# A new order, new engine places and new buffer slots for a two-layer attention and MLP kernel on one core

## The chip, the core and the metric

The kernel runs on one core of a Trainium2 chip. A core has five engines with queues of their own: TensorE (PE in the profile; PEld is its weight load), VectorE (DVE), ScalarE (ACT), GpSimd (POOL) and SyncE (SP, which here issues transfers). Each engine works through its own instructions in program order and waits on semaphores for the others. The metric is the device time of one execution in microseconds (us); a smaller number is better.

## The reference

The input x (2048 tokens, 512 wide, bfloat16) passes twice through an attention layer A and a gated MLP layer B with the same weights:

```
def A(x):                                  # 32 heads of 16
    q, k, v = heads(layernorm(x) @ wqkv)
    pq, pk = q @ w_phi, k @ w_phi          # per head, 16 x 16
    phi_q = concat(softmax(pq), softmax(-pq));  phi_k = concat(softmax(pk), softmax(-pk))
    kv, z = phi_k^T @ v, sum(phi_k)        # over all tokens
    return (phi_q @ kv / (phi_q @ z + 1e-6)) @ wo
def B(x):
    gate, up = layernorm(x) @ W_gate, layernorm(x) @ W_up     # 512 -> 1376
    return (relu(gate) * up) @ W_down
x = x + A(x);  x = x + B(x);  x = x + A(x);  x = x + B(x)
```

Since kv and z are sums over all tokens, no query of a layer can be finished before the keys of all 16 tiles of that layer are.

## The kernel before

The tokens are 16 tiles of 128. x stays in on-chip memory (X0 to X3, four tiles each) through both layers. The work on a tile in layer A is: statistics (L508, L509), the inverse deviation on ACT (L516, L518), the normalised tile (L532 on DVE or L530 on POOL), a transpose (by a DMA at L493, in pairs of tiles, or for a few tiles by PE at L498 with a copy at L451 on ACT or L452 on DVE), then keys (K, L600) and values (V, L605). Before the first keys the kernel folds w_phi into the key and query weights (L471 and L479 on PE; the folded block matrix Wblk comes from L427). The keys are exponentiated on ACT (`ek`, L572), summed on DVE (L610), inverted through a logarithm and an exponential on ACT (L619, L622), scaled on DVE or POOL (L559), and multiplied with the values (L633) into one sum for all tiles; L645 and L650 make the matrix R of it on DVE.

A query goes the same way: Q (L660), exponentials (L572), a sum on DVE (L665), its inverse on ACT (L670, L672), a ratio on DVE (L676), a scaling on DVE or POOL (L681), and a DMA transpose into a buffer `fq` (L685). PE then multiplies it with R (L696, called `erq` below, "the read of a query"); the denominator is inverted (L705 on DVE, or L703 and L707 on ACT), the result divided (`o`, L710 on DVE), transposed by DMA in pairs of tiles (`oT`, L493; L498 by PE for the first tiles) and projected with wo (L719); L723 adds it to x.

Layer B takes blocks of 1, 1, 2, 4, 4, 2, 2 tiles in the first layer and 1, 1, 2, 4, 4, 2, 1, 1 in the second. A block is centred (L739), transposed (`xnTB`, L493), and multiplied with gate and up weights (L796; L772 does the last 96 columns for both, whose product `hr` is transposed by a DMA at L823 into the buffer `hT`). ACT takes the relu (L800); the product with up is made on DVE straight from PSUM (L813) or, after a copy of up by ACT (L815), from on-chip memory (L804). The sum of squares is taken on ACT (L745) or on DVE (L747). L836 multiplies with W_down, L843 adds to x, and in the second layer L909 stores the tile.

All of this is recorded first as 1882 operations. Three tables, found beforehand by a search and written into the file, then decide how they run:

- `ORDER` is the order in which the recorded operations are emitted; each engine's own program is that order cut down to its operations.
- `PLACE` has one digit for each operation that two engines can do, and says whether it goes to the other one (POOL or DVE for L427, L530/L532, L559 and L681; ACT or DVE for copies out of PSUM, the product of gate and up, the sum of squares and the denominators; the SP or ACT queue for a few loads).
- `SLOTS` says which buffer of its pool each operation takes: six PSUM banks `b`, seven `fq`, three `xn`, two `o`, three `oT`, and so on. A later user of a slot waits for the former one's last reader.

All transposes, nearly all loads and all stores are issued from SP, in one queue: an issue that waits for its input holds up every one behind it.

Of the kernel before, what the change touches and what calls it, by code (L numbers as in the profile page):

```python
# [145 lines left out]
class K:  # L146
# [9 lines left out]
    "1100101010111011000101001001110000010000110100110101011100110100011100000001000001110111001100010011"  # L156
    "1011110010100110100110101100110010000011011000100110000101000000000000000010011101011011010000001111"
    "0110100011101101110101110000000000111100101110110100110101000000011111100110000101111000110000101110"
    "0000100111111000101101011000101101111011000011010111100"
)  # L160
SLOTS = (
    "0001451253130010000013433322441511022214304534304520050102235401411130832125312102411256331270021370"
    "4314410132122a2009024c310d231b142h251i001a160j315f152c0209233g122e344k001d36000505011414020002510110"
    "2031000011100000200102101214001021540100022005020051044205021251402023121002134234005118130100014100"
    "2202135243040120423155003011400413211322102300425203200113411011250122634200130057121522132001013152"
    "0101100530350341111442332040341322131322140103k3135j4101150021153235201052103215i3413442210011100400"
    "020112511430024103022325032b063h232a104i354j212c0219345b232c364e203h220a335f0419364g112d150115040202"
    "1200101212020000200110211000001242011020510000120100015021011410003214302515421031152025013100015005"
    "2133051131225042310241140520100300510201110131221041032244530110101030112103012251121021125251220055"
    "30120011510440022320332204103111211515311001500000542450235"  # L170
# [784 lines left out]
```

## Time and profile before

| what | value |
|---|---|
| median of 3 runs | 371.1 us (370.42 to 371.11) |
| the profiled execution | 371.12 us, of which the span of the instructions is 369.1 us |
| PE busy | 362.4 us, 98% of the span |
| DVE busy | 260.5 us, 71% |
| ACT busy | 197.3 us, 53% |
| POOL busy | 70.0 us, 19% |
| granted TensorE clock | 0.999 of full speed, mean |
| moved by DMA | 31.73 MB, of it 0.36 MB and 0.11 MB on the two queues that the page calls instruction |

A profile row names a line of the kernel, an engine, an operation, and what it writes and reads (out<-in, buffer numbers left out). A row of the timeline begins with the start of the first instruction and the time it covers, both in us; the bracket at its end gives the idle time of the engine before it and what ended it. "SPq" is an issue on SP's queue, its second number the time that the issue took. Times of PE overlap: a matmul of 512 columns lasts 379 ns from start to modelled end, while the next one begins 216 ns after it.

### The profile page before, as it was taken

The numbers are of one execution on the slowest core, as the hardware profiler recorded it, in microseconds if no ns is written. First come the engines' busy times: TensorE is split into PE (matmuls) and PEld (weight loads), VectorE is DVE, ScalarE is ACT, GpSimd is POOL, SyncE is SP. The second block draws the span as 40 slices with busy tenths as digits, with TensorE's granted clock in tenths as the row PEclk, the third lists the DMA queues.
The fourth block names the chain that finished last, engine by engine and source line by source line (L and its number), as shares of the span: only waits on it lengthen the run. The fifth ranks groups of instructions, "written<-read, shape, count | busy, mean of one in ns | idle before, by whom it ended". The sixth has DMA issues, their size and how long they took to land.

```text
span 369.1 us, 7462 instructions
## 1 busy us (share of the span) xinstructions
PE 362.4 (98%) x2845; PEld 217.2 (59%) x2845; DVE 260.5 (71%) x598; ACT 197.3 (53%) x562; POOL 70.0 (19%) x99
## 2 busy tenths in 40 slices
PE   8989999999999999999999999999999999999996
PEld 5545567776455544456767455777744444466684
DVE  6989999999667457657959878898845823432343
ACT  5989998645256531655555477854422431323231
POOL 4688930320200000003002671040010000000000
PEclk9999999999999999999999999999999999999999
DMA  7998486556544400221012611156861110202013
GB/s 221 252 191 204 180 133 126 106 114 142 115 89 73 95 1 2 44 66 28 2 36 59 143 30 30 29 117 133 138 118 30 43 28 2 57 16 65 16 46 119
DMA packets 93923, 31.73 MB, mean 86 GB/s; under 512 B 85344, under 2 KB 92864, under 8 KB 93888
## 3 DMA queue, kind: packets, MB, share of 16 engines
q1 hardware_dynamic: 93888, 31.26, 38.6%
q8 instruction: 22, 0.36, 0.4%
q14 instruction: 13, 0.11, 0.1%
HBM read 8.44 MB, written 2.10 MB: 29 GB/s over the span
## 4 chain that ended last, share of the span: by engine, by line
PE 84%; DMA 7%; DVE 4%; SPq 2%; ACT 1%; issue 1%
PE b L796 34%; PE b L836 18%; PE b L719 7%; PE b L605 6%; PE b L600 6%; PE b L660 6%; PE b L772 2%; DMA fq<-ek 2%; PE q L633 2%; DMA oT<-o 2%; PE q L696 2%; DMA xnTA<-xn 1%; DVE sq L665 1%; DMA X<-in_A_x_dram 1%; PE b L498 1%; DVE X L723 1%
## 5 line engine op out<-in xcount | busy, mean ns | idle before, releaser
L796 PE MATMUL b<-xnTB,wgu 128*128 128x128 bf16 (+2 forms) x1200 | 153.4, 279 | 0.0
L796 PEld LDWEIGHTS <-wgu 128*128 128x128 bf16 x1200 | 97.4, 98 | 46.1 <-issue 0.2
L800 ACT ACTIVATE gu<-b 128x512 bf16<-128x512 f32 (+1 forms) x83 | 47.5, 581 | 105.9 <-PE b L796 104.6
L836 PE MATMUL b<-wd,hT 128*128 128x512 bf16 (+3 forms) x363 | 85.2, 373 | 0.1
L572 ACT ACTIVATE ek<-b 128x480 bf16<-128x480 f32 x128 | 68.9, 580 | 12.8 <-PE b L600 6.7
L813 DVE TENSOR_TENSOR hT<-gu,b 128x512 bf16<-128x512 bf16 (+1 forms) x49 | 32.8, 671 | 38.2 <-PE b L796 19.0
L836 PEld LDWEIGHTS <-hT 128*128 128x128 bf16 (+1 forms) x363 | 34.6, 98 | 35.5 <-DMA hT<-hr 0.6
L681 POOL TENSOR_TENSOR ek<-ek 128x480 bf16<-128x480 bf16 x19 | 18.6, 990 | 158.2 <-DVE ek L676 82.5
L559 POOL TENSOR_TENSOR ek<-ek 128x480 bf16<-128x480 bf16 x39 | 38.7, 1016 | 34.2 <-ACT ek L622 33.6
L665 DVE TENSOR_REDUCE sq<-ek 128x64 f32<-128x960 bf16 x32 | 36.3, 1143 | 1.0 <-ACT ek L572 1.0
L610 DVE TENSOR_REDUCE sk<-ek 128x64 f32<-128x960 bf16 x32 | 36.0, 1142 | 1.0 <-ACT ek L572 0.7
L843 DVE SCALAR_TENSOR_TENSOR X<-b,rsB,X 128x512 bf16<-128x512 f32 (+2 forms) x33 | 24.1, 730 | 12.3 <-PE b L836 12.2
L723 DVE SCALAR_TENSOR_TENSOR X<-b,X 128x512 bf16<-128x512 f32 x32 | 21.7, 684 | 15.1 <-PE b L719 15.0
L719 PE MATMUL b<-wo,oT 128*128 128x512 bf16 x128 | 31.9, 379 | 0.5 <-DMA oT<-o 0.4
L605 PE MATMUL b<-wv,xnTA 128*128 128x512 bf16 x128 | 31.5, 379 | 0.0
L600 PE MATMUL b<-Wk,xnTA 128*128 128x480 bf16 x124 | 28.9, 366 | 1.7 <-DMA xnTA<-xn 1.7
L660 PE MATMUL b<-Wq,xnTA 128*128 128x480 bf16 x128 | 30.0, 366 | 0.0
L710 DVE TENSOR_TENSOR o<-q,rd 128x512 bf16<-128x512 f32 x32 | 22.0, 688 | 5.3 <-ACT rd L707 4.8
L508 DVE BATCH_NORM_STATS2 bstA<-X 128x6 f32<-128x512 bf16 x32 | 21.3, 682 | 2.0 <-DMA X<-in_A_x_dram 1.8
L815 ACT CAST gu<-b 128x512 bf16<-128x512 f32 (+1 forms) x34 | 18.8, 560 | 6.2 <-PE b L796 6.0
L804 DVE TENSOR_TENSOR hT<-gu 128x512 bf16<-128x512 bf16 (+1 forms) x34 | 13.6, 402 | 11.2 <-ACT gu L815 10.9
L600 PEld LDWEIGHTS <-xnTA 128*128 128x128 bf16 x124 | 11.7, 98 | 13.9 <-DMA xnTA<-xn 1.8
(81 smaller groups left out, 333.5 us busy)
## 6 DMA issues: line engine op xcount, KB each, us to landing
out_dram<-X SPq DMA_DIRECT2D x15, 128.0 KB, 1.8
X<-in_A_x_dram SPq DMA_DIRECT2D x6, 256.0 KB, 5.0
wgu<-in_B_W_gate_dram SPq DMA_DIRECT2D x4, 344.0 KB, 4.5
wgu<-in_B_W_up_dram SPq DMA_DIRECT2D x4, 344.0 KB, 5.8
wd<-in_B_W_down_dram SPq DMA_DIRECT2D x5, 256.0 KB, 3.6
hT<-in_A_wqkv_dram SPq DMA_DIRECT2D x4, 256.0 KB, 4.0
X<-in_A_x_dram SPq DMA_DIRECT2D x4, 128.0 KB, 3.0
wv<-in_A_wqkv_dram SPq DMA_DIRECT2D x2, 256.0 KB, 4.4
```

What stands on the lines that cost most here:

```text
L559: e.tensor_tensor(out=v[:, :, 0:DF, :], in0=v[:, :, 0:DF, :], in1=spread(ek, v, n), op=Alu.mult)
L572: nc.scalar.activation(out=pairs(ek, s)[:, :, 0:DF, :], in_=ps.t[:, 0:FW].rearrange("p (b f h) -> p b f h", h=2, f=DF), func=AF.Exp, scale ...
L600: k = op("PE", mm(4, FW), due, lambda: [nc.tensor.matmul(kp.t[:, 0:FW], lhsT=xnTA[c][:, i, b, :], rhs=Wk2[:, b, :], start=(b == 0), stop=( ...
L605: v = op("PE", mm(4, 512), due_v, lambda: [nc.tensor.matmul(vp.t[:], lhsT=xnTA[c][:, i, b, :], rhs=wv[:, b, :], start=(b == 0), stop=(b == ...
L610: a = op("DVE", SUM16, due, lambda: nc.vector.tensor_reduce(out=sk.t[:, row, :].rearrange("p (b h) -> p b h", h=2), in_=summed(pairs(ek)), ...
L660: q = op("PE", mm(4, FW), due, lambda: [nc.tensor.matmul(qp.t[:, 0:FW], lhsT=xnTA[c][:, i, b, :], rhs=Wq2[:, b, :], start=(b == 0), stop=( ...
L665: a = op("DVE", SUM16, due, lambda: nc.vector.tensor_reduce(out=sq.t[:].rearrange("p (b h) -> p b h", h=2), in_=summed(pairs(ek)), axis=AX ...
L719: a = op("PE", mm(4, 512), due + 3, lambda j=j, yp=yp: [nc.tensor.matmul(yp.t[:], lhsT=oT.t[:, j, b, :], rhs=wo[:, b, :], start=(b == 0), ...
L796: nc.tensor.matmul(ps.t[:, q * W:(q + 1) * W].rearrange("p (i t) -> p i t", t=P), lhsT=wgu[:, s, b, g * P:(g + 1) * P], rhs=xT.t[:, 0:n, b ...
L800: nc.scalar.activation(out=gu.t[:, 0, 0:cols], in_=gp.t[:, 0:cols], func=AF.Relu)
L813: nc.vector.tensor_tensor(out=h.t[:, f0 * W:f0 * W + cols], in0=gu.t[:, 0, 0:cols], in1=up.t[:, 0:cols], op=Alu.mult)
L836: nc.tensor.matmul(yp.t[:, 0:c1 - c0], lhsT=h.t[:m, f * W + i * P:f * W + (i + 1) * P], rhs=wd[:m, f, c0:c1], start=(f == 0), stop=(f == N ...
```

## The change

The three tables are replaced. No operation is added or removed, and no other line differs: the 2845 matmuls are the same ones, and so are the widths and the blocks. The first rows of each table:

```diff
 PLACE = (
-    "1100101010111011000101001001110000010000110100110101011100110100011100000001000001110111001100010011"
+    "1110001010101011000100001101110100010000110100000001011000010110001111001001000001011100001100001100"
...
 SLOTS = (
-    "0001451253130010000013433322441511022214304534304520050102235401411130832125312102411256331270021370"
+    "0001451040132010500014430222331211020213005544034243050301110131332321832325222114330207421163021150"
...
 ORDER = (
-    2, 16, 9, 29, 3, 21, 25, 0, 8, 4, 102, 1, 10, 103, 17, 19, 22, 104, 7, 105, 46, 30, 106, 32, 5, 31, 47, 6, 84, 48,
+    3, 16, 9, 29, 2, 0, 17, 19, 25, 8, 4, 1, 10, 102, 6, 103, 30, 46, 7, 104, 32, 105, 106, 31, 5, 47, 84, 48, 14, 49,
```

What `PLACE` moves, counted over the operations: 6 of 64 key scalings (L559) and 6 of 32 query scalings (L681) go from POOL to DVE; the block matrix Wblk (L427) goes from POOL to DVE; one normalised tile from POOL (L530) to DVE (L532); three sums of squares from ACT (L745) to DVE (L747); three products of gate and up from DVE alone (L813) to ACT and DVE (L815, L804); one more denominator goes to ACT; one weight load goes from the SP queue to the ACT queue. PE's program has as many instructions as before.

Three places show how the order differs. The first is the queue of SP at the start, from the last early load to the transpose of the second pair of tiles (`xn2` into `xnTA3`); `hT0` holds the query weights there, `hT1` their transpose. Before:

```order
L353 DMA wd_71<-in_B_W_down_dram 96x512
L493 DMA_TRANSPOSE xnTA1_80<-xn0_109 128x8x128
L869 DMA hT0_163<-in_A_wqkv_dram 128x2x512
L465 DMA_TRANSPOSE hT1_164<-hT0_163 128x8x128
L353 DMA wo_66<-in_A_wo_dram 128x512
L353 DMA X2_63<-in_A_x_dram 128x2x512
L493 DMA_TRANSPOSE xnTA3_82<-xn2_111 128x8x128
```

and now:

```order
L353 DMA wo_66<-in_A_wo_dram 128x512
L493 DMA_TRANSPOSE xnTA1_80<-xn0_109 128x8x128
L353 DMA X3_64<-in_A_x_dram 128x2x512
L869 DMA hT0_163<-in_A_wqkv_dram 128x2x512
L465 DMA_TRANSPOSE hT1_164<-hT0_163 128x8x128
L493 DMA_TRANSPOSE xnTA3_82<-xn2_111 128x8x128
```

Between the two transposes of x there are now three other issues and not four; the load of `wo` stands ahead of both.

The second place is on DVE, where the eighth `o` of the first layer is made; the seventh projection of PE waits for it. Before:

```order
L710 TENSOR_TENSOR o0_156<-q0_102,rd0_153 128x512
L843 SCALAR_TENSOR_TENSOR X0_61<-b1_104,rsB0_96,X0_61 128x512
L804 TENSOR_TENSOR hT1_164<-gu2_167 128x512
L676 SCALAR_TENSOR_TENSOR ek19_131<-sq3_145 128x16x2
L681 TENSOR_TENSOR ek19_131<-ek19_131 128x16x30
L676 SCALAR_TENSOR_TENSOR ek9_121<-sq2_144 128x16x2
L754 SCALAR_TENSOR_TENSOR sqB0_95<-ssq_84,lnB0_97 128x1
L676 SCALAR_TENSOR_TENSOR ek20_132<-sq0_142 128x16x2
L705 RECIPROCAL rd1_154<-q0_102 128x32
L781 TENSOR_TENSOR hr0_170<-gr1_169,b2_105 128x96
L710 TENSOR_TENSOR o0_156<-q0_102,rd1_154 128x512
```

and now:

```order
L710 TENSOR_TENSOR o0_156<-q0_102,rd0_153 128x512
L804 TENSOR_TENSOR hT0_163<-gu2_167 128x512
L532 TENSOR_SCALAR xn0_109<-X0_61,mvA1_92,rsA1_93 128x512
L751 TENSOR_TENSOR lnB0_97<-rowsum_83 128x2
L723 SCALAR_TENSOR_TENSOR X1_62,rowsum_83<-b2_105,X1_62 128x512
L747 SCALAR_TENSOR_TENSOR wasteD_86,ssq_84<-X0_61 128x512
L723 SCALAR_TENSOR_TENSOR X1_62,rowsum_83<-b5_108,X1_62 128x512
L754 SCALAR_TENSOR_TENSOR sqB0_95<-ssq_84,lnB0_97 128x2
L804 TENSOR_TENSOR hT0_163<-gu0_165 128x512
L705 RECIPROCAL rd1_154<-q0_102 128x32
L710 TENSOR_TENSOR o0_156<-q0_102,rd1_154 128x512
```

Between the seventh and the eighth `o` there are now two additions to x (L723), a sum of squares (L747) and a normalised tile of the next layer (L532), each 512 wide.

The third place is the queue of SP in the attention of the second layer, up to the transpose of the query of tile 11. That query goes into `fq3` before and into `fq5` now. Before:

```order
L493 DMA_TRANSPOSE oT2_160<-o0_156 128x8x128
L493 DMA_TRANSPOSE xnTB0_161<-xn1_110 128x8x128
L685 DMA_TRANSPOSE fq4_150<-ek15_127 128x8x128
L493 DMA_TRANSPOSE oT0_158<-o1_157 128x4x128
L493 DMA_TRANSPOSE xnTB0_161<-xn2_111 128x8x128
L493 DMA_TRANSPOSE oT1_159<-o0_156 128x4x128
L685 DMA_TRANSPOSE fq3_149<-ek10_122 128x8x128
```

and now:

```order
L685 DMA_TRANSPOSE fq3_149<-ek12_124 128x8x128
L685 DMA_TRANSPOSE fq6_152<-ek14_126 128x8x128
L685 DMA_TRANSPOSE fq5_151<-ek16_128 128x8x128
L493 DMA_TRANSPOSE oT0_158<-o0_156 128x8x128
L685 DMA_TRANSPOSE fq2_148<-ek11_123 128x8x128
L493 DMA_TRANSPOSE oT2_160<-o1_157 128x4x128
L493 DMA_TRANSPOSE xnTB0_161<-xn0_109 128x8x128
```

The transpose of that query stood behind three transposes of `o` and two of `xn` and was the last of the seven; it now stands ahead of both transposes of `o` and of the transpose of `xn` in the piece shown.

More of the change, by code (lines that the diff above doesn't have):

```diff
@@ L155 @@
 PLACE = (
-    "1100101010111011000101001001110000010000110100110101011100110100011100000001000001110111001100010011"
-    "1011110010100110100110101100110010000011011000100110000101000000000000000010011101011011010000001111"
-    "0110100011101101110101110000000000111100101110110100110101000000011111100110000101111000110000101110"
-    "0000100111111000101101011000101101111011000011010111100"
+    "1110001010101011000100001101110100010000110100000001011000010110001111001001000001011100001100001100"
@@ L160 @@
+    "1111010101001111110000100000110110011010010101100000100011000100100000011100111100010000100010111110"
+    "1110001011110100001010100000110011100100101001111100101100010101011011111000110100110110100111000100"
+    "0010000100011010011111011001000111111100101110100100001"
 )
 SLOTS = (
-    "0001451253130010000013433322441511022214304534304520050102235401411130832125312102411256331270021370"
-    "4314410132122a2009024c310d231b142h251i001a160j315f152c0209233g122e344k001d36000505011414020002510110"
@@ L164 @@
[L164 to L168, printed above, removed]
@@ L169 @@
-    "2133051131225042310241140520100300510201110131221041032244530110101030112103012251121021125251220055"
-    "30120011510440022320332204103111211515311001500000542450235"
+    "0001451040132010500014430222331211020213005544034243050301110131332321832325222114330207421163021150"
+    "43375021032559100a020c214d141b332h054f362c105k231i3549013a320g141e203j165b01000000011111020002530110"
+    "2052000011050000204202101213001021020100001400010001042032225056210020141101113100001013443103004200"
+    "5024102252034024832130232211211001211414305400512015021500501424203120233311431134500254221004105021"
@@ L171 @@
+    "02015020100312401021224420100230221701026341142312581332141121113251055111242400k5433334000000400550"
+    "4123310521121425400211j0213d222h110f303c033a065k2559325f311d101g145b323g155i002a210c032e260114210204"
+    "1100101010020002320110212400001034011022530000104100011021210011114014020514023010050015242135111114"
+    "0112013132253124000220001300002341212232511021352150000541521101013132122010250142250053200130123002"
+    "05310400520232022520411404202003012523313501311300121120432"
 )
```

178 rows, old and new, of the table ORDER are left out of this document.

## The prediction, as put on record

> **What bounds the kernel now.** I read the page first, then the timeline of PE for every place where it stands still, then the chain of waits for the cause of each.
>
> ```profile
> PE 362.4 (98%) x2845; PEld 217.2 (59%) x2845; DVE 260.5 (71%) x598; ACT 197.3 (53%) x562; POOL 70.0 (19%) x99
> DVE  6989999999667457657959878898845823432343
> ```
>
> PE is busy for 98% of the span, and the change leaves its 2845 matmuls as they are. So the end can move only by what PE loses in standing still. The second line says where another engine is close to being the bound: DVE is at 90% or more of most slices (9.2 us each) up to 90 us, and far from it after that. The places where PE stands still are few. Each pair below is the group before the wait and the group that waited:
>
> ```profile
> 18.56 0.42 PE L633 MATMUL q<-vext,ek 128*128 128x65 bf16 x8
> 20.67 0.98 PE L600 MATMUL b<-Wk,xnTA 128*128 128x480 bf16 x4 [1.69 <-DMA xnTA<-xn]
> ...
> 52.79 1.78 PE L660 MATMUL b<-Wq,xnTA 128*128 128x480 bf16 x8
> 54.65 0.43 PE L696 MATMUL q<-R,fq 128*128 128x68 bf16 x8
> ...
> 78.34 0.42 PE L696 MATMUL q<-R,fq 128*128 128x68 bf16 x8
> 78.85 1.90 PE L719 MATMUL b<-wo,oT 128*128 128x512 bf16 x8
> ...
> 85.85 1.03 PE L719 MATMUL b<-wo,oT 128*128 128x512 bf16 x4
> ...
> 255.25 0.42 PE L696 MATMUL q<-R,fq 128*128 128x68 bf16 x8
> 256.05 1.04 PE L719 MATMUL b<-wo,oT 128*128 128x512 bf16 x4 [0.39 <-DMA oT<-o]
> ...
> 269.86 1.68 PE L836 MATMUL b<-wd,hT 128*128 128x512 bf16 x7
> 272.01 0.43 PE L696 MATMUL q<-R,fq 128*128 128x68 bf16 x8 [0.47 <-DMA fq<-ek]
> ...
> 361.84 4.39 PE L836 MATMUL b<-wd,hT 128*128 128x512 bf16 x29
> ```
>
> A group's covered time runs about 0.16 us past the moment at which the next could start (379 ns of life against a pitch of 216), so the next was due at start + time - 0.16. The six waits are then 20.67 - 18.82 = 1.85, 54.65 - 54.41 = 0.24, 78.85 - 78.60 = 0.25, 256.05 - 255.51 = 0.54, 272.01 - 271.38 = 0.63, and one inside the last group, which the chain of waits shows:
>
> ```profile
> 75.67 3.13 DMA oT<-o
> ...
> 361.14 2.24 DMA hT<-hr
> 363.43 2.19 PE b L836 x12
> ```
>
> Six matmuls after 361.84 would end at 363.14; the seventh needs the transpose issued at 361.14 and starts at 363.43: 0.29. Together 3.8 us, all of them transposes by DMA. That is most of what a new order can win; what it can lose has no such limit. The chain also gives 3.13 us from the issue of an `oT` to PE's use of it.
>
> **Why the transposes came late.** On SP at the start, and at two of the late places:
>
> ```profile
> 11.08 1.32 SPq L493 DMA_TRANSPOSE xnTA<-xn  x1
> 12.46 1.61 SPq L869 DMA_DIRECT2D hT<-in_A_wqkv_dram  x1
> 14.17 1.24 SPq L465 DMA_TRANSPOSE hT<-hT  x1
> 15.45 0.60 SPq L353 DMA_DIRECT2D wo<-in_A_wo_dram  x1
> 16.59 1.24 SPq L493 DMA_TRANSPOSE xnTA<-xn  x1
> ...
> 250.60 2.11 SPq L685 DMA_TRANSPOSE fq<-ek  x1
> 264.04 1.55 SPq L493 DMA_TRANSPOSE oT<-o  x1
> ```
>
> A load of the same size as the one at 12.46 is issued in about 0.5, a transpose in 1.24; these took 1.61, 2.11 and 1.55. In the window 12 to 14 us the DMA view has one packet on the instruction queue:
>
> ```profile
> q8 instruction: 1, 0.02, 3.5%
> ```
>
> So an issue held up in the presence of an instruction fetch is a thing of this trace, and everything behind it in SP's queue is late: at 256 the `oT` stood right behind the issue of 2.11, at 272 the query's transpose stood behind the held `oT`.
>
> **Part 1, the start.** The transpose that ends the first wait now has one load of wo fewer between it and the transpose before it: -0.60 by the row at 15.45. Against that, DVE makes the block matrix ahead of the first `xn` of that queue. The trace has no such row on DVE; the bounds are the POOL row of the same operation, 1.02, and a DVE multiplication of the same width, 0.48.
>
> ```profile
> L427 POOL TENSOR_TENSOR Wblk<-wd,Mf 128x480 bf16<-128x480 bf16 x1 | 1.0, 1017 | 1.7 <-DVE vext L408 1.7
> L559 DVE TENSOR_TENSOR ek<-ek 128x480 bf16<-128x480 bf16 x25 | 11.3, 478 | 2.8 <-ACT ek L622 2.8
> L452 DVE CAST Wk<-b 128x480 bf16<-128x480 f32 x1 | 0.7, 658 | 0.0
> L452 DVE CAST vext<-b 128x512 bf16<-128x512 f32 x7 | 4.7, 680 | 1.6 <-PE b L605 1.6
> L532 DVE TENSOR_SCALAR xn<-X,mvA,rsA 128x512 bf16<-128x512 bf16 x21 | 9.0, 442 | 2.7 <-ACT rsA L518 2.5
> L804 DVE TENSOR_TENSOR hT<-gu 128x512 bf16<-128x512 bf16 x30 | 12.5, 418 | 11.2 <-ACT gu L815 10.9
> L705 DVE RECIPROCAL rd<-q 128x32 f32<-128x32 f32 x17 | 6.0, 354 | 2.8 <-PE q L696 2.7
> L723 DVE SCALAR_TENSOR_TENSOR X<-b,X 128x512 bf16<-128x512 f32 x32 | 21.7, 684 | 15.1 <-PE b L719 15.0
> L747 DVE SCALAR_TENSOR_TENSOR wasteD<-X 128x512 bf16<-128x512 bf16 x6 | 4.1, 677 | 0.1
> ```
>
> I take the multiplication: the same kind on the same engine. One weight cast fewer (0.66) and one copy more (0.42, as wide as L804) leave +0.2, +0.8 at the dear end; one load gone from SP to ACT's queue lets the first tiles land up to 0.4 earlier. Net 0.1 late, so the first wait ends 0.5 earlier, between 0.9 earlier and 0.2 later.
>
> **That gain does not reach the end,** because the second read of a query is bound by DVE already:
>
> ```profile
> 49.68 0.18 DVE L676 SCALAR_TENSOR_TENSOR ek<-sq 128x32 bf16<-128x32 f32 x1
> ...
> 49.94 0.99 POOL L681 TENSOR_TENSOR ek<-ek 128x480 bf16<-128x480 bf16 x1 [1.35 <-DVE ek L676]
> ...
> 48.82 4.93 SPq L685 DMA_TRANSPOSE fq<-ek  x3
> ...
> 21.91 0.66 DVE L452 CAST Wq<-b 128x480 bf16<-128x480 f32 x1 [0.99 <-PE b L479]
> ```
>
> The ratio at 49.68, the scaling on POOL that ends at 50.93, and the middle one of three transposes set the 54.65. In the new order the same ratio has these more ahead of it on DVE: Wblk 0.48, two key scalings 0.96, one tile 0.44, one copy 0.42, one ratio 0.18; and fewer: one cast of Wk 0.66, one of V 0.68, one query scaling 0.48. That is +0.66, or +1.2 with Wblk at POOL's price. DVE's idle 0.99 at 21.91, behind PE's first wait, should mostly go, as the fold that it waits for comes 0.5 earlier and more work stands ahead of that cast. I take +0.2, from -0.3 to +1.2. PE also does four small transposes ahead of this read that stood behind it (about 0.2 of its own work), so **what is left of the start is 0.0**.
>
> **Part 2, DVE between 50 and 90 us.** Ahead of the eighth `o` the new order has more on DVE: two L723 1.37, two L747 1.35, three L804 1.25, three L705 1.06, two L559 0.96, two L532 0.88; what else was added and dropped cancels to 0.1. Sum 6.9; since neighbours overlap by about 0.08 and there are 14 instructions more, at least 5.8. Before, that `o` and the idle time there were:
>
> ```profile
> 80.00 0.69 DVE L710 TENSOR_TENSOR o<-q,rd 128x512 bf16<-128x512 f32 x1
> ...
> 50.00:80.00 30.00, 29.84 (x375) 22.21 (x372) 27.64 (x70) 23.20 (x73) 5.10 (x6) 1.00 0.71 128
> ```
>
> DVE was busy for 27.64 of 30, so 2.36 us can take up some of it. The `o` ends between 80.69 + 5.8 - 2.36 = 84.1 and 80.69 + 6.9 = 87.6, and is at PE 3.13 later: 87.2 to 90.7. The seventh projection began at 85.85; it now has 3.25 us more matmul work ahead of it since the second read (by PE's rows and their pitches), and the 0.25 of 78.85 lies in between: PE is there at 88.85. The wait is 0 to 1.9. I take 0.5, nearer the low end, since the waits of DVE in this stretch are for PE and ACT and go when its queue is longer.
>
> **Part 3, the four later waits.** At 272 the query's transpose now stands ahead of the transposes of `o` that held it up. At 78.85 two transposes of queries that stood ahead of the `oT` now stand behind it. At 256 the `oT` stands ahead of the query transpose that was held for 2.11. At the end the last 96-column group of the second to last tile is computed some 2.6 us of matmul work earlier. So 0.25 + 0.54 + 0.63 + 0.29 = 1.71 goes. New ones can come: between the read of tile 7 and its projection in the second layer lie 6.4 us of matmuls instead of 7.1, against 0.35 + 0.69 + 3.13 for the denominator, `o` and transpose. I take 0.3, from 0 to 1.7 (as many as before).
>
> **Sum** against the profiled execution's 371.12 (the median is 371.1, so nothing is to be added): 0.0 + 0.5 + 0.3 - 1.71 = -0.9, **370.2 us**.
>
> **The rivals.**
>
> *DVE becomes the bound (slower).* The eighth `o` ends at 87.6, PE loses 1.9 at the seventh projection, and DVE does not recover: it is over the next projections as well, so I add 0.5 to 1 for the ninth, with the late waits as above: 1.9 + 0.75 + 0.3 - 1.71 = +1.2, 372.3. For it speak the 6.9 us and the slices at 9; against it that the idle 2.36 and 22.92 busy of the 30 us after 80 give room. It decides from the point where that `o` ends after 85.8 (88.85 - 3.13).
>
> *The late waits come back elsewhere (no change).* Waits behind other transposes belong to a queue with 138 rows, whatever their order; with 1.7 new ones and no wait at the seventh projection the sum is 0.0: 371.1. The Trainium skill speaks for this rival: "Runtime: NRT & Kernel Launch", section "Instruction fetch mechanics", says that an engine's sequencer fetches the next 16 KiB block itself while it works on the present one, and that the cost is mostly hidden. By that rule an order that avoids fetches wins nothing and the time stays. The held issues above speak against the rule as far as SP goes: 0.3 to 1.1 us each.
>
> *All of it is won (faster by more).* The second read comes 0.3 earlier, PE's four transposes count, and nothing new waits: -0.3 - 0.2 - 1.71 = -2.2, 368.9. Against it: every part has to fall at its good end.
>
> **How the numbers follow.** This kernel's runs tell 0.2% (0.74 us) from no change. The forecast has 0.46: its sum lies just beyond that bound, and I give 0.36 to faster and 0.10 to the same. DVE as the bound has 0.31 (0.28 slower, 0.03 same), the late waits coming back 0.16 (0.14 same, 0.02 slower), all of it won 0.07. That makes faster 0.43, same 0.27, slower 0.30. The forecast's own range is 369.6 to 371.0. The range for 8 in 10 runs from 369.0, the point where all is won, to 372.8, DVE as the bound with half a us more at a second place.
>
> **What would show it.** Part 1: the first transposed tile at K is waited for by about 1.2, and the second read of a query starts at 54.3 to 55.5 all the same. Part 2: DVE busy over 29 of the 30 us from 50 to 80, and an idle of PE before the seventh projection of about 0.5 near 89. Part 3: no wait of PE over 0.4 after 100 us, and none before the last 12 matmuls. I am wrong if PE waits on DVE for over 2 us before 110 us, or if waits on `oT`, `fq` or `xnTB` after 100 us come to more than 1.2.

## The result, and the profile after

| | before | changed |
|---|---|---|
| median, 20 runs each | 371.01 us (369.95 to 374.12) | 369.7 us (369.33 to 370.73) |
| ratio to before, with its 95% interval | 1 | 0.9964 (0.9952 to 0.9976) |
| the profiled execution | 371.12 us, span 369.1 | 369.7 us, span 367.9 |

The changed kernel is 1.3 us (0.36%) faster by the medians, where 0.9 was forecast. The page of the changed kernel, its first two parts and a row of the third:

```profile
span 367.9 us, 7455 instructions
...
PE 362.1 (98%) x2845; PEld 217.1 (59%) x2845; DVE 264.5 (72%) x617; ACT 196.6 (53%) x561; POOL 56.6 (15%) x84
...
DVE  6999999999886656656799897896874553353415
...
q8 instruction: 22, 0.36, 0.4%
```

PE is as busy as before, POOL has 13.4 us less and DVE 4.0 more (260.5 before). The eleventh and twelfth slice of DVE (92 to 110 us) stand at 8 where 6 stood before. Where PE stands still is in its timeline:

```profile
14.27 0.97 PE L600 MATMUL b<-Wk,xnTA 128*128 128x480 bf16 x4
15.86 0.98 PE L600 MATMUL b<-Wk,xnTA 128*128 128x480 bf16 x4 [0.62 <-ACT vext L451]
...
53.45 0.39 PE L498 MATMUL b<-ident,o 128*128 128x128 bf16 x4
53.67 0.42 PE L696 MATMUL q<-R,fq 128*128 128x68 bf16 x8
...
87.06 1.02 PE L836 MATMUL b<-wd,hT 128*128 128x512 bf16 x4
87.92 1.89 PE L719 MATMUL b<-wo,oT 128*128 128x512 bf16 x8
...
247.94 1.68 PE L836 MATMUL b<-wd,hT 128*128 128x512 bf16 x7
250.86 1.04 PE L719 MATMUL b<-wo,oT 128*128 128x512 bf16 x4 [1.25 <-DMA oT<-o]
```

With the prediction's rule (start + covered time - 0.16 is when the next was due) there is a wait of 0.78 at 15.86, none at the second read (53.67) and at the seventh projection (87.92), and one of 1.40 at 250.86. Four small ones of 0.1 to 0.2 stand at 22, 57, 124 and 232 us. That makes about 2.7 where the kernel before has 3.8, and the span is 1.2 shorter. All four late waits of before are gone; the one at 250.86 is new and almost as large as they were together (1.71).

What happened there is read from three views of the changed kernel: SP's queue, the chain of waits, and DMA from 248.5 to 251 us (40 columns of 0.06 us each).

```profile
244.58 1.23 SPq L823 DMA_TRANSPOSE hT<-hr  x1
245.90 1.26 SPq L493 DMA_TRANSPOSE oT<-o  x1
247.25 1.41 SPq L493 DMA_TRANSPOSE xnTB<-xn  x1
```

```profile
245.90 4.92 DMA oT<-o
250.81 0.05 issue
```

```profile
GB/s 123 229 250 274 287 516 229 188 45 74 78 0 0 0 0 0 0 0 0 0 8 4 12 4 12 8 12 8 8 12 8 12 98 283 279 303 279 307 279 214
...
q8 instruction: 1, 0.02, 2.4%
```

No issue was held. The transpose was issued in time but took 4.92 us to land, where those between 60 and 110 us take 3.0 to 3.2. The one instruction packet in that window lies at 248.81 to 249.77; from 249.2 to 250.5 DMA moves 0 to 12 GB/s, and then about 280 again. By this view a fetch holds not only an issue, as the prediction had it, but also a transpose that is already under way. The runs below that move the fetches test it.

At the start, SP's queue in the changed kernel:

```profile
11.31 1.33 SPq L493 DMA_TRANSPOSE xnTA<-xn  x1
...
13.87 2.02 SPq L465 DMA_TRANSPOSE hT<-hT  x1
15.98 1.36 SPq L493 DMA_TRANSPOSE xnTA<-xn  x1
```

The first fetch (13.58 to 14.77) falls on the transpose issued at 11.31, which takes 4.5 to land, and holds the issue at 13.87. The keys at 15.86 need that transpose, landed at 15.8, and a PSUM bank that ACT frees at the same moment. The second transpose of x (15.98, before 16.59) lands 3.06 after its issue, where it took 4.03 before, and is in time for its keys at 19.69.

On DVE, the ratio of the second read, the eighth `o`, and the busy time from 50 to 80 us (columns as in the prediction):

```profile
49.32 0.19 DVE L676 SCALAR_TENSOR_TENSOR ek<-sq 128x32 bf16<-128x32 f32 x1
...
82.86 0.69 DVE L710 TENSOR_TENSOR o<-q,rd 128x512 bf16<-128x512 f32 x1
...
50.00:80.00 30.00, 30.00 (x349) 22.26 (x346) 28.93 (x73) 21.53 (x66) 4.48 (x5) 1.00 0.56 107
```

The ratio comes 0.36 earlier than before (49.68), and the eighth `o` ends at 83.55. From the start of the kernel to the end of that `o` DVE is busy for this long, before and now (its figure is the third one behind the comma):

```profile
0.00:80.70 80.70, 77.82 (x731) 48.41 (x732) 73.53 (x157) 67.63 (x208) 41.99 (x71) 1.00 0.75 172
...
0.00:83.56 83.56, 81.94 (x770) 52.04 (x771) 78.24 (x176) 67.16 (x204) 38.11 (x66) 1.00 0.71 170
```

### The profile page after: what moved, and what is told of

It reads as the page before. It is cut to its first block, busy times and chain, and to the rows that moved or that the text cites. A ratio compares the mean times of both kernels' runs of the same rounds, so it can differ in the third digit from the quotient of the medians.

```text
span 367.9 us, 7455 instructions
## 1 busy us (share of the span) xinstructions
PE 362.1 (98%) x2845; PEld 217.1 (59%) x2845; DVE 264.5 (72%) x617; ACT 196.6 (53%) x561; POOL 56.6 (15%) x84
## 4 chain that ended last, share of the span: by engine, by line
PE 96%; DMA 1%; ACT 1%; DVE 0%; issue 0%
PE b L796 38%; PE b L836 20%; PE b L719 8%; PE b L605 7%; PE b L660 7%; PE b L600 6%; PE b L772 3%; PE q L696 2%; PE q L633 2%; DMA oT<-o 1%; PE q L445 1%; PE b L498 1%; ACT ek L572 1%; PE b L479 0%; PE b L471 0%; DVE X L843 0%
## 5 line engine op out<-in xcount | busy, mean ns | idle before, releaser
L813 DVE TENSOR_TENSOR hT<-gu,b 128x512 bf16<-128x512 bf16 (+1 forms) x46 | 30.9, 676 | 33.3 <-PE b L796 19.4
L559 POOL TENSOR_TENSOR ek<-ek 128x480 bf16<-128x480 bf16 x33 | 32.9, 1023 | 127.0 <-ACT sq L670 56.4
L804 DVE TENSOR_TENSOR hT<-gu 128x512 bf16<-128x512 bf16 (+1 forms) x37 | 14.8, 401 | 18.0 <-ACT gu L815 17.8
L815 ACT CAST gu<-b 128x512 bf16<-128x512 f32 (+1 forms) x37 | 20.2, 555 | 12.3 <-PE b L796 12.3
L723 DVE SCALAR_TENSOR_TENSOR X<-b,X 128x512 bf16<-128x512 f32 x32 | 21.8, 684 | 3.8 <-PE b L719 3.6
L681 POOL TENSOR_TENSOR ek<-ek 128x480 bf16<-128x480 bf16 x13 | 12.9, 994 | 51.3 <-DVE ek L676 48.0
L719 PEld LDWEIGHTS <-oT 128*128 128x128 bf16 x128 | 11.8, 98 | 13.4 <-DMA oT<-o 1.9
```

Source lines behind the costliest of these rows:

```text
L559: e.tensor_tensor(out=v[:, :, 0:DF, :], in0=v[:, :, 0:DF, :], in1=spread(ek, v, n), op=Alu.mult)
L719: a = op("PE", mm(4, 512), due + 3, lambda j=j, yp=yp: [nc.tensor.matmul(yp.t[:], lhsT=oT.t[:, j, b, :], rhs=wo[:, b, :], start=(b == 0), ...
L813: nc.vector.tensor_tensor(out=h.t[:, f0 * W:f0 * W + cols], in0=gu.t[:, 0, 0:cols], in1=up.t[:, 0:cols], op=Alu.mult)
```

## The experiments

Two questions were open: why the start's gain reached the end though the second read was thought to be bound by DVE, and whether a fetch is the cause of the waits or only stands beside them. Ratios are to the kernel before, measured on the same chip.

| run | edit | median us | ratio (95%) |
|---|---|---|---|
| e1_ot_first | changed: one `oT` issue earlier | 369.01 | 0.9934 (0.9911 to 0.9957) |
| e2_v_first | changed: V ahead of K at the start | 369.51 | 0.9947 (0.9929 to 0.9965) |
| e3_warm90 | changed: 90 PE instructions more | 369.84 | 0.9955 (0.9934 to 0.9977) |
| e4_warm54 | changed: 54 PE instructions more | 369.9 | 0.9956 (0.9934 to 0.9977) |
| e5_before_wo_first | before: a load of wo earlier | 370.89 | 0.999 (0.9979 to 1.0001) |
| e6_after_wo_back | changed: a load of wo later | 370.28 | 0.9975 (0.9959 to 0.9991) |
| e7_ot_hr_first | changed: `oT` and `hr` issues earlier | 368.56 | 0.9929 (0.9917 to 0.9941) |
| e8_before_warm54 | before: 54 PE instructions more | 372.02 | 1.003 (1.0014 to 1.0046) |
| e9_dve_more | changed: 6.8 us more on DVE | 373.32 | 1.0052 (1.0033 to 1.007) |
| e10_both | changed: e7, V first, a load later | 368.24 | 0.9914 (0.9886 to 0.9942) |

### The fetches moved, the tables untouched

The page has 22 packets on the instruction queue and 5690 instructions on PE (2845 matmuls and as many weight loads): one packet for every 259. So a few more PE instructions at the start, in the place of the matmuls that warm PE up, should move every later fetch to another place in the work. The stretch of these matmuls lasts 4.00 us with either number of them. On the kernel before (e8_before_warm54) and the changed one (e4_warm54):

```diff
-    op("PE", (3630, 3800, 9), 0, lambda: idle(9), (), [wps], name="warm")
+    op("PE", (3630, 3800, 36), 0, lambda: [nc.tensor.matmul(wps.t[0:32].rearrange("p g e -> p (g e)")[:, 0:128], lhsT=one[
+        :, 0:32], rhs=one[:, 0:128], start=True, stop=True) for _ in range(36)], (), [wps], name="warm")
```

For e8_before_warm54 was expected:

> The kernel before, with the 9 warming matmuls replaced by 36 of 128 columns: 54 PE instructions more, its tables untouched. Theory F: each fetch comes some 54 PE instructions earlier in the work (the late ones 2 to 3 us); the issues held before at 12.46, 250.60 and 264.04 are not held any more, others are; the first wait at 20.67 and the waits at 256.05 and 272.01 change by 0.3 or more each, in either direction, and the time moves by up to 1.5 us: ratio 0.996 to 1.003. Rival N (the waits belong to the order of the queue, not to the fetches): the same waits at the same places within 0.2, ratio 0.9995 to 1.0005.

In its timeline of PE and its chain of waits:

```profile
20.71 0.98 PE L600 MATMUL b<-Wk,xnTA 128*128 128x480 bf16 x4 [1.06 <-DMA xnTA<-xn]
...
78.12 0.42 PE L696 MATMUL q<-R,fq 128*128 128x68 bf16 x8
80.19 1.90 PE L719 MATMUL b<-wo,oT 128*128 128x512 bf16 x7 [1.64 <-DMA oT<-o]
...
273.21 0.43 PE L696 MATMUL q<-R,fq 128*128 128x68 bf16 x8 [0.67 <-DMA fq<-ek]
```

```profile
75.45 4.69 DMA oT<-o
80.14 0.04 issue
```

The fetch that lay at 79.82 before, where no transpose was under way, lies at 76.50 now, in the middle of this `oT`: it lands after 4.69 instead of 3.1, and a wait of 0.25 has become 1.81 (80.19 - 78.38). The wait at 256 shrank from 0.54 to 0.22, the one at 272 (here 273.21) grew from 0.63 to 0.83, less than the 0.3 that F named. The first one is 1.2 instead of 1.85, but that says nothing: it ends at 20.71, as before (20.67), and PE came to it 0.7 later, 0.5 of it from the first 10 us. At the first reads of the queries PE is where it was before (52.57 against 52.53), so the loss comes behind them. No row of the tables differs, so N falls, and F holds where it counts: the waits belong to the place of the fetches as much as to the order. The kernel before had a rather good place; this one is 0.3% slower.

The same edit on the changed kernel, and one with 54 matmuls of 84 columns (e3_warm90):

> The changed kernel, with the 9 warming matmuls at the start (512 columns, results unused) replaced by 54 of 84 columns with 32-column weights: 90 PE instructions more ahead of all work, about as much time. Theory F (one fetch on the instruction queue for each 256 PE instructions): every fetch comes 90 PE instructions earlier in the work. The first, at 13.58, moves to about 7 us, where no transpose is in flight, so the wait at 15.86 (0.78 of lateness) goes; the one at 248.81 moves to about 245.1, ahead of the issue of the transpose of o at 245.90, so the wait at 250.86 (1.41) falls to under 0.5. Waits of up to 0.5 can come at other places, so the time is 0.8 to 2 us less than the changed kernel's, ratio 0.991 to 0.994. Rival N (transposes issued next to each other slow each other, and the fetch only stands beside them): the fetches move but the waits at 15.86 and 250.86 stay within 0.3 us of what they were, ratio 0.996.

> As the run before, with 36 warming matmuls of 128 columns: 54 PE instructions more. Theory F: the first fetch moves to about 9 us and the wait at 15.86 goes (0.78 less); the late one moves to about 246.1, into the first half of the same transpose of o, which is still held: a wait of 0.4 to 1.5 us stays near 250. Ratio 0.993 to 0.9955. Rival N: both waits stay within 0.3 us of what they were, ratio 0.996.

SP's and PE's rows of e3_warm90:

```profile
243.66 2.81 SPq L823 DMA_TRANSPOSE hT<-hr  x1
246.57 1.26 SPq L493 DMA_TRANSPOSE oT<-o  x1
```

```profile
249.86 1.04 PE L719 MATMUL b<-wo,oT 128*128 128x512 bf16 x4 [1.17 <-DMA oT<-o]
...
261.18 0.43 PE L696 MATMUL q<-R,fq 128*128 128x68 bf16 x8 [1.03 <-DMA fq<-ek]
```

In both the wait at 15.86 is gone, as F said, though the first fetch came at 10.64 and 12.49 and not near 7 and 9. In e4_warm54 it held the issue of the first transpose of x for 1.0 more, and a wait of 0.62 came at 20.08 instead. The late part missed. In e3_warm90 the fetch came at 243.66, not 245.1, held the issue of `hr` for 1.6 more, and with it the `oT` behind it: a wait of 1.3 stayed at 249.86, as rival N had it. The next fetch, at 257.48, fell on a query transpose, and a new wait of 1.2 came at 261.18; one of 0.5 came at 278.75. In e4_warm54 the fetch came at 247.0, on the issue of that `oT` (1.93 instead of 1.26), which landed in 3.5: the wait at 250 vanished, where F had 0.4 to 1.5, and waits of 0.76 at 278 and 0.53 at 348 came instead. So F's mechanism is borne out by where the waits went, and its sizes are not to be had from counting instructions to within a microsecond. Both ratios came out near N's 0.996, and neither time can be told from the changed kernel's.

### The late wait taken away by the order

If the fetch near 248.8 is the cause, what it falls on should have time to spare. e1_ot_first moves the `oT` (operation 1402) ahead of a query's transpose (1301) that is needed 12 us later:

```diff
-    1492, 1497, 1399, 1400, 1292, 1508, 1515, 1488, 1516, 1392, 1493, 1401, 1324, 1518, 1522, 1301, 1363, 1340, 1353,
-    1354, 1341, 1390, 1499, 1407, 1498, 1521, 1393, 1402, 1391, 1526, 1500, 1537, 1528, 1539, 1408, 1409, 1540, 1529,
+    1492, 1497, 1399, 1400, 1292, 1508, 1515, 1488, 1516, 1392, 1493, 1401, 1324, 1518, 1522, 1402, 1301, 1363, 1340,
+    1353, 1354, 1341, 1390, 1499, 1407, 1498, 1521, 1393, 1391, 1526, 1500, 1537, 1528, 1539, 1408, 1409, 1540, 1529,
```

> The changed kernel, with one issue of SP moved: the transpose of o that PE waits for at 250.86 (1.25 us idle) is issued ahead of one query transpose, about 2.6 us earlier (243.3 instead of 245.90). Theory F (instruction fetch): that transpose landed 4.92 us after its issue because the fetch of PE's instructions at 248.81 fell on it; issued at 243.3 it lands by 246.6, the fetch then falls on transposes with over 3 us to spare, the wait at 250.86 is gone and nothing takes its place: 1.2 to 1.4 us less than the changed kernel, ratio to the kernel before 0.9925 to 0.9935. Rival P (lateness is passed on: the tail of the attention is bound by DVE and SP together): a wait of 0.7 us or more stands at one of the next projections or at the first matmuls of the next block, and the time falls by less than 0.7 us.

SP's and PE's rows of e1_ot_first:

```profile
243.12 1.25 SPq L493 DMA_TRANSPOSE oT<-o  x1
244.48 1.28 SPq L685 DMA_TRANSPOSE fq<-ek  x1
245.81 1.22 SPq L823 DMA_TRANSPOSE hT<-hr  x1
```

```profile
250.30 0.39 PE L836 MATMUL b<-wd,hT 96*128 96x512 bf16 x1 [1.05 <-DMA hT<-hr]
```

The `oT` landed in 3.3 us, but the move had pushed the transpose of `hr` from 244.58 to 245.81, where the fetch (247.86 here) met it: 4.4 to land, where others take 2.4, and a wait of 1.2 on it. By this wait it was rival P's outcome, by its mechanism F's. The ratio (0.9934) lies in F's range, but its interval (0.9911 to 0.9957) reaches the changed kernel's, and the profiled execution is only 0.4 shorter (369.33). e7_ot_hr_first puts the query's transpose behind both (1301 behind 1499):

> The changed kernel, with one query transpose of SP (issued at 243.28, needed at 255.26) put behind the transposes of o and of hr that follow it. In the run that moved only the transpose of o, that one landed in 3.3 us, but the transpose of hr was pushed back to 245.81, took the fetch at 247.86 and landed 4.45 later, for a wait of 1.22. Theory F: here o is issued near 243.2 and hr near 244.5, both land before the fetch near 248, which falls on the query transpose with over 4 us to spare and on the transpose of xn behind it: the wait near 250 falls from 1.41 to under 0.5, ratio 0.9925 to 0.994. Rival P (lateness is passed on): a wait of over 0.9 stands there again, behind another transfer, ratio 0.995 to 0.9965.

SP's and PE's rows of e7_ot_hr_first:

```profile
243.04 1.25 SPq L493 DMA_TRANSPOSE oT<-o  x1
244.34 1.23 SPq L823 DMA_TRANSPOSE hT<-hr  x1
245.67 1.25 SPq L685 DMA_TRANSPOSE fq<-ek  x1
```

```profile
248.13 1.24 PE L836 MATMUL b<-wd,hT 128*128 128x512 bf16 x5
249.22 1.03 PE L719 MATMUL b<-wo,oT 128*128 128x512 bf16 x4
```

The projection starts as soon as PE is there (248.13 + 1.24 - 0.16), with the fetch at 248.06. The query's transpose takes 4.5 to land in its place, and nothing waits for it. Its interval (0.9917 to 0.9941) lies clear of the changed kernel's: two issues of SP that change places, with a third left between them, are worth as much again as the whole change.

### Whether the start's gain reaches the end

> The kernel before, with one issue of SP moved: the load of wo that stands between the two transposes of x at the start goes ahead of both, as the change has it. The transpose issued at 16.59 comes 0.6 earlier and PE's first wait at 20.67 (1.85) falls to about 1.2. Theory S (the start's gain reaches the end): PE is 0.4 to 0.6 earlier at the second read of a query too, ratio about 0.9985. Rival D (the prediction's: DVE binds the second read): that read still starts at 54.4 or later, its wait grows from 0.24 to 0.6 or more, ratio 0.9995 to 1.0005. Either way the waits at 256 and 272 stay unless the instruction fetches fall elsewhere.

The edit moves operation 294, a load of wo, ahead of operation 128, the first transpose, in the table of the kernel before. PE's and DVE's rows of e5_before_wo_first:

```profile
19.74 0.98 PE L600 MATMUL b<-Wk,xnTA 128*128 128x480 bf16 x4 [0.39 <-DMA xnTA<-xn]
...
53.64 0.43 PE L696 MATMUL q<-R,fq 128*128 128x68 bf16 x8
```

```profile
20.98 0.66 DVE L452 CAST Wq<-b 128x480 bf16<-128x480 f32 x1 [0.26 <-PE b L479]
...
48.72 0.18 DVE L676 SCALAR_TENSOR_TENSOR ek<-sq 128x32 bf16<-128x32 f32 x1
```

DVE's work and its order are those of before, yet the ratio stands at 48.72 instead of 49.68, and the second read at 53.64 instead of 54.65, with a wait of 0.2 as before. DVE's queue waited for PE at 21.91 (0.99 idle); with PE's first wait ending 0.93 earlier (19.74 against 20.67) that idle is 0.26, and everything behind it on DVE comes earlier too. D falls by the trace. The times alone would not say so: the ratio (0.999) lies between those of S and D, and its interval covers both. The span is 0.8 shorter (368.3) in the profiled execution, the median 0.33 (370.89 against 371.22 of before on the same chip), and part was given back at 271.48, where the wait for a query's transpose grew from 0.63 to 1.08.

The reverse on the changed kernel puts operation 273, a load of wo, behind operation 326, the transpose of query weights:

> The changed kernel, with the load of wo put back between the two transposes of x, where the kernel before has one. The transpose issued at 15.98 comes 0.6 later and is then used at 19.69 + 0 to 0.3; a wait of 0 to 0.6 comes there. Theory S: what is lost at the start is lost at the end, ratio 0.9964 to 0.998. Rival D: the loss is taken up by the second read, ratio 0.9964.

PE's row shows what it cost:

```profile
23.82 0.38 PE L479 MATMUL b<-Wblk,hT 128*128 128x120 bf16 x4 [0.40 <-DMA hT<-hT]
```

The wait came not at the keys but at the fold behind the second transpose of the query weights, 0.56 where the changed kernel has 0.12. The profiled execution lost 1.1 us more before the edit's place (a load that landed late at 8 us). Beyond that, PE is 0.4 later at the first read of a query and 0.2 later at the end, so part of the loss stayed. The median is the better witness of the time: 0.0011 above the changed kernel's ratio, within the intervals. It agrees with S and proves little.

e2_v_first moves operation 76 (values) ahead of 142 (keys):

> The changed kernel, with one operation of PE moved: the values of a tile that is ready (V, the row at 16.68) are computed ahead of the keys that PE waits for at 15.86 (0.62 us idle, 0.78 of lateness). Theory S (the start's gain reaches the end): the wait at 15.86 is covered by 0.86 us of work and goes, PE is 0.6 to 0.8 us earlier from there to the end, ratio to the kernel before about 0.9945. Rival D (the prediction's: the second read of a query is bound by DVE): the wait at 15.86 goes, the second read still starts at 53.5 or later and waits 0.5 to 0.8 us for its transpose, and the time stays: ratio 0.996 to 0.997.

```profile
15.78 1.02 PE L605 MATMUL b<-wv,xnTA 128*128 128x512 bf16 x4
...
22.98 0.38 PE L479 MATMUL b<-Wblk,hT 128*128 128x120 bf16 x4 [0.69 <-DMA hT<-hT]
```

The wait at the keys went, and the same fold waited 0.85: neither S nor D, but a third thing, the next transfer of the same queue. Its time can't be told from the changed kernel's. e10_both adds to e7 that move and puts operation 13, a load of x, behind that transpose (327):

> The changed kernel with the two moves of SP that took the late wait away (the transposes of o and of hr ahead of a query transpose), with the values of a ready tile ahead of the keys that wait at 15.86, and with one load of x (256 KB) put behind the second transpose of the query weights, which was what the run with the values first waited for at 22.98 (0.85). Theory S (the start's gain reaches the end, waits are chained only through SP's queue): no wait over 0.3 between 10 and 60 us, none near 250; PE is 2.7 to 3.3 us behind its bare work at the end, ratio 0.990 to 0.992. Rival P (another transfer of the start takes the place of the one moved): a wait of 0.4 to 0.9 comes at the keys or at the fold between 19 and 24 us, ratio 0.992 to 0.994.

No wait over 0.3 was left between 10 and 60 us, and none near 250; of the 0.63 that e7 loses at 15.86, waits of 0.2 at 15.62 and 25.37 remain. Its first 10 us cost 0.2 more in the profiled execution, and its span (366.4) is no shorter than that of e7 (366.2). The two can't be told apart; both are faster than the changed kernel.

### Whether DVE is the bound

```diff
-                alt=("DVE", RESSUM, lambda t=t: nc.vector.scalar_tensor_tensor(
+                alt=("DVE", RESSUM, lambda t=t: [nc.vector.scalar_tensor_tensor(
                     out=wasteD[:], in0=x_of(t), scalar=1.0, in1=x_of(t), op0=Alu.mult, op1=Alu.mult,
-                    accum_out=ssq[:, l, t:t + 1]), True)))
+                    accum_out=ssq[:, l, t:t + 1]) for _ in range(1 if l else 3)], True)))
```

> The changed kernel, with each sum of squares that DVE takes in the first layer (four of them, two of them ahead of the eighth o) computed three times over, the same values each time: 8 instructions of 0.61 us more on DVE between 74 and 200 us, 2.4 us of them ahead of the eighth o, which ended at 83.55 and was transposed with 0.69 us to spare for the projection at 87.92. Theory R (DVE has become the bound between 50 and 90 us, as the prediction's first rival had it): DVE's 1.07 us of idle time from 50 to 80 do not help, that o ends 2.4 later, PE waits 1.7 at the seventh projection and more behind it, and the time is 1.7 us or more longer: ratio 1.001 or more. Theory M (DVE is full but behind a margin): part of the 2.4 goes into DVE's idle time, the seventh projection waits 0.2 to 1.0, and nothing of the like after 100 us: 0.2 to 1.0 longer, ratio 0.997 to 0.999.

PE's rows of e9_dve_more, and its windows:

```profile
79.08 1.89 PE L719 MATMUL b<-wo,oT 128*128 128x512 bf16 x7 [0.47 <-ACT gu L800]
85.51 1.03 PE L796 MATMUL b<-xnTB,wgu 128*128 128x256 bf16 x8 [1.66 <-DVE X L723]
```

```profile
50.00:80.00 30.00, 29.32 (x352) 22.18 (x353) 28.87 (x72) 20.86 (x64) 4.86 (x5) 1.00 0.52 102
```

PE lost 0.63 at 79 and 1.82 at 85.5, 2.45 in all, for four instructions that kept DVE busy 2.9 us longer (three sums take 2.1, one takes 0.6). The first layer has five such sums, not four, so the edit added ten instructions and 6.8 us (271.3 busy against 264.5). The two near 127 and 132 cost 0.1, the one at 158 cost 1.0. The median is 3.6 above the changed kernel's; by the ratios, each to the kernel before on the same chip, it is 3.3. So theory R holds in its size: what DVE gets more between 70 and 90 us PE loses almost in full. That is so at these places and not everywhere, as the two sums near 130 show. The place of the waits was another than expected. It was not the seventh projection but the gate and up products ahead of it, which wait for a PSUM bank until DVE has made the addition L723, queued behind the repeated sums.

## Why the prediction was right, and where it was wrong

The time (369.7 against 370.2) and the direction were right, but the time is right in part by luck: three of the four terms were wrong, the start by 1.2 and DVE by 0.5 on the pessimistic side, the new late waits by 1.4 on the optimistic side.

- **The first wait** was to end 0.5 earlier (0.9 earlier to 0.2 later). The wait on the second transpose went altogether, and 0.78 at 15.86 and 0.12 at 22 came: 0.95 earlier. The transpose was issued 0.61 earlier, as the removed load (0.6) has it. That it also landed 3.06 after its issue instead of 4.03 was no term of the sum, and no run shows the reason.
- **"That gain does not reach the end"** is the step that failed. It set the second read's time by DVE's work ahead of its ratio (+0.66) and gave back only part of DVE's idle time. In fact the ratio came 0.36 earlier, not 0.2 later. The durations of that work did grow by 0.6, but neighbours overlap, so DVE's busy time before the ratio grew by 0.2 only (44.87 to 45.10); the prediction took overlap off in part 2 and not here. And DVE's idle time before it fell from 4.8 to 4.2. Most of that was not the 0.99 at 21.91, of which 0.80 is left (at 22.83), but waits beside it (from 10 us on, 1.8 in all before and 1.1 now). e5_before_wo_first shows the gain pass through DVE without any change of DVE's work. With the wait of 0.24 the start brought 1.2, not 0.0.
- **DVE between 50 and 90** was to cost 0.5 and cost nothing. The eighth `o` ended at 83.55, below the predicted 84.1 to 87.6. DVE entered the stretch 0.36 earlier with PE, and the work added ahead of that `o` takes 4.7 us (73.53 to 78.24), not 5.8 to 6.9: the durations grew by 6.5, of which 1.8 overlap, where the prediction allowed for 1.1. 1.07 of its 2.36 us of idle time were left. That DVE is nearly the bound there, as the first rival had it, is right by e9_dve_more.
- **The four late waits** went, 1.71 as predicted. Whether the moves that the prediction named took them away, or the places of the fetches, no run separates: in e3_warm90 and e4_warm54 the new order has late waits at places where the changed kernel has none. The new ones came to 1.7, at the top of the bounds (0 to 1.7), not 0.3. That is the rival of the late waits coming back, by one wait and not many, and for a reason the prediction saw only half of: it counted issues held by a fetch, not transposes held under way.

So the terms were 0.0 + 0.5 + 0.3 - 1.71 = -0.9, and the trace has -1.2 + 0 + 1.7 - 1.7 = -1.2. Of the marks that were named, "none before the last 12 matmuls" came out, and DVE's 29 of 30 us nearly did (28.93). The 1.2 at the first transposed tile, the second read at 54.3 to 55.5 (it starts at 53.67), the 0.5 near 89 and "no wait over 0.4 after 100 us" did not. By its own measure (1.2 us of waits on such transposes after 100 us, where there are 1.6) the reasoning was wrong in the late part, though the time was right.

The Trainium skill, "Runtime: NRT & Kernel Launch", section "Instruction fetch mechanics", says that an engine's instructions come in blocks of 256. The trace's 259 PE instructions for each packet agree. The same section of the Trainium skill calls the cost of crossing a block mostly hidden. For PE itself no run shows a wait on its instructions; for a transpose by DMA that is under way, the waits of 1.4 and 1.8 above disagree.

What stays open: why a fetch holds a whole transpose. The packet itself takes 0.9 to 1.8 us, about as long as the delay. That one of the DMA engines which carry the transpose is busy with the packet and the others wait for it would fit the near-zero traffic, but no run tested it.

## What to carry to other kernels

A gain at the start of an in-order queue that has an idle gap behind the same wait moves the whole queue: before saying "bound by the other engine", find what that engine itself waited for. Where transposes by DMA are on the path, list the fetches (here one for 259 PE instructions) beside them, and put transfers with microseconds to spare under the fetches. When an order is judged by one trace, also move the fetches, by a few PE instructions at the start: here their places alone made 0.3% (e8_before_warm54), nearly as much as the whole change of the tables (0.36%).

## What the runs showed of the hardware

The spread of landing times over the whole changed kernel, for the transposes of `hr`, then of the queries:

```profile
DMA to landing us min/median/max: 2.2/2.4/4.3
...
DMA to landing us min/median/max: 2.7/2.8/5.5
```

The median lies close to the minimum, and the long ones are those that meet an instruction packet. Past 45 us, in all twelve profiled executions, these are the times from issue to landing of transposes that met no packet of either instruction queue, and of those that met a 16 KB packet (of the queue q8) at some moment of that time:

| transpose | met none | median, longest us | met one | median, longest us |
|---|---|---|---|---|
| `o` | 116 | 3.1, 3.3 | 52 | 4.4, 5.1 |
| `hr` | 133 | 2.4, 2.6 | 41 | 3.4, 4.4 |
| a query | 237 | 2.8, 3.3 | 101 | 4.3, 5.7 |
| `xnTB` | 133 | 2.7, 3.0 | 28 | 3.9, 4.6 |

Of the 619 that met none, none took over 3.4 us. The 8 KB packets of the second instruction queue hold transposes too: 46 queries that met only one of these took 3.5 in the median. An issue that meets a packet took up to 2.81 in the rows above instead of 1.24. And the profiled executions differ by over 1 us in their first 10 us: the first product with the value weights began at 9.63 in the changed kernel, and at 10.69 in e6_after_wo_back, where PE waited 1.01 for a load at 8.07.
